# One step for a head pair's sums over values, and one pool of four PSUM banks for experts and values

## Chip, cores and metric

The kernel runs on one core of one Trainium2 chip. The metric is the device time of one execution in microseconds. Before the change three runs took 910.35, 912.54 and 912.85 us, a median of 912.54 us.

## What is computed

Eight batches of eight heads, 576 positions, head size 64. Causal attention with a decay that is summed from `f`; its rows go, 512 values per position (8 heads of 64), into a layer that takes the largest of three products and multiplies it by a fourth matrix. Cut to what matters:

```python
scores = q @ k.T / sqrt(64) + cum[i] - cum[j]        # cum = cumsum(log(clip(f)))
attn   = softmax over j <= i of scores               # 64 heads (8 batches x 8), 576 x 576
out    = attn @ v
x      = out laid out as 4608 tokens x 512
h      = max(x @ w1, x @ w2, x @ w3)                 # 512 -> 768
result = h @ w_out                                   # 768 -> 512
```

## The kernel before

**A plan writes the order.** Nothing is run as it is written. Every piece of work is handed to `Plan.add` (line 68) as a step: an engine, a cost in nanoseconds, a function that issues its instructions, the keys it reads and writes, and a priority. `Plan.emit` (line 87) then plays the steps through a model of the five engines: each engine takes, of the steps whose inputs are ready, the one with the lowest rank (priority less a small weight for the work that hangs on it). The order in which steps begin in that model is the order in which their instructions are issued. On the chip the engines run these queues in order, and semaphores on the data hold them. Steps of TensorE may carry two marks: `short` (a score pass whose last block is so narrow that the weight load behind it is not covered by it) and `light` (a step whose weights are 64 columns wide). After a `short` step the model looks for a `light` one (lines 117 to 128).

**Scores.** `scores` (line 646) handles a head in two units: unit 2 is the first 256 queries, unit 1 the other 320 (`UNITS`, line 610). In each, keys are on the partitions and queries on the columns, in blocks of up to 128 keys. A pass A (TensorE, line 675) fills the unit's PSUM banks, VectorE and GpSimd find a maximum (lines 730 to 748), a pass B (line 675 again) subtracts it, ScalarE takes exponentials (line 763) into a buffer of probabilities. Batch 0 (n below 8) has a form of its own that the change leaves as it is. Heads 8 to 15 have two such buffers for each unit, later heads three (`probs`, line 641).

**Values.** From head 8 on, two heads make a pair. `values` calls `values_pair` (line 820) once for unit 1 and once for unit 2, 28 pairs and so 56 steps. A step multiplies the probabilities of both heads by their values: the two heads fill the upper and the lower 64 partitions of one PSUM bank, `t` (`TPS`, line 373), with weights 64 columns wide, so that the two heads' matmuls run side by side (line 831). Unit 1 takes 20 matmuls, unit 2 takes 8. ScalarE copies the bank to `u` (line 858), and the other unit waits for that copy, since there is one bank. For heads 8 to 15 the row sums are taken in the same bank by a further step of 32-column matmuls (line 850) and copied by line 856; for later heads GpSimd sums them (line 787). `finish_pair` (line 942) divides: small DMAs through `sc` and `rdram` spread the reciprocal of the sums over a tile `r`, and VectorE multiplies `u` by it (line 961). When a batch is done `split_x` (line 963) writes its four `u` tiles as a high part (ScalarE, line 966) and a low part (VectorE, line 968).

**Experts.** `moe` runs batch b's layer while batch b+1's attention runs. `gemm1` (line 980) makes a group of 12 matmuls of 256 or 320 columns (line 992) for each of the three matrices; ScalarE copies the first (line 999), VectorE takes the maximum with the other two (line 1001), then the result is split (lines 1004, 1006). `gemm2_part` (line 1015) makes a group of 18 matmuls (line 1021), which ScalarE copies to `o` (line 1028). A group takes the next of three banks `mp0` to `mp2` in turn:

```python
def next_mp():                       # line 975
    i = mcount[0] % NM               # NM = 3
    mcount[0] += 1
    return MPS[i], f"mp{i}"
```

All transfers go through SyncE's queue, in the order of the plan.

Of the kernel before, what the change touches and what calls it, by code (L numbers as in the profile page):

```python
# [47 lines left out]

class Plan:
# [15 lines left out]
    def __init__(self):  # L65
        self.steps, self.wrote, self.read, self.parts = [], {}, {}, {}

    def add(self, eng, cost, fn, r=(), w=(), prio=0.0, xfer=0.0, rows=128, short=0.0, light=False):
# [16 lines left out]
        self.steps.append((eng, cost, fn, deps, prio, xfer, rows, short, light))  # L85

    def emit(self):
# [22 lines left out]
        clock = GatedClock()  # L110
        while done < n:
            best = None
            for e in free:
                t = free[e] if live[e] else (max(free[e], wait[e][0][0]) if wait[e] else None)
                if t is not None and (best is None or t < best[0]):
                    best = (t, e)
# [5 lines left out]
            here = live[e][0]  # L122
            if e == "PE" and (short or self.steps[here[1]][8]):


                x = min((x for x in live[e] if (self.steps[x[1]][8] if short else not self.steps[x[1]][8])), default=here)
                if x[0] < here[0] + (self.LIKE if short else self.HOLD):
                    here = x
# [9 lines left out]
            begin[i] = t  # L138
            cost = (self.steps[i][1] - saved) * self.ROOM[e][0] + self.ROOM[e][1]
# [5 lines left out]
            if self.steps[i][5]:  # L145
                moved = max(moved, end + 650) + self.steps[i][5]
                end = moved + self.LATE
                lanes.append(end + 650)
            for u in users[i]:
# [31 lines left out]
def kernel(  # L181
# [15 lines left out]
    nc = tc.nc  # L197
# [148 lines left out]
    def ZR():  # L346
        return lazy("rx", [P, 384], F32)
# [442 lines left out]
    def values(n, unit, prio):  # L790
# [26 lines left out]
        if j:  # L817
            values_pair(n, unit, prio)

    def values_pair(n, unit, prio):  # L820

        pi, d, t, kt = n // 2, UNITS[unit], TPS, "t0"
        u = pi % NU
        q0, nq, cols = d["q0"], d["nq"], d["cols"]
        vn, kv = VN[vbuf(pi)], f"vn{vbuf(pi)}"
        prs = [probs(n - 1, unit), probs(n, unit)]
# [8 lines left out]
        wide = n < WIDE  # L835
        add("PE", sum(4.04 * x[2] / 2.4 for x in cols) + 250, go, [k for _, k in prs] + [kv], [kt], prio, light=True)
        if wide:

            half, z0 = nq // 2, nq
            runs = [[(max(qa, half * a), min(qa + w, half * a + half), col - qa) for c, qa, w, col in cols] for a in range(2)]  # L840
            runs = [[x for x in xs if x[0] < x[1]] for xs in runs]

            def total():
                for x in range(max(map(len, runs))):
                    for j in range(2):
                        for a in range(2):
                            if x < len(runs[a]):
                                qa, qe, col = runs[a][x]
                                r = 64 * j + 32 * a
                                nc.tensor.matmul(  # L850
                                    t[r:r + 32, z0 + qa - half * a:z0 + qe - half * a], ZR()[:, 288:320],
                                    prs[j][0]()[:, col + qa:col + qe], start=False, stop=True, skip_group_check=True)

            add("PE", max(sum(4.04 * (x[1] - x[0]) / 2.4 for x in xs) for xs in runs) + 100, total,
                [k for _, k in prs] + ["ones", kt], [kt], prio)
            add("ACT", act_cost(half), lambda: nc.scalar.activation(
                ZR()[:, 128 * (2 - unit):128 * (2 - unit) + half], t[:, z0:z0 + half], AF.Copy), [kt], [f"zr{unit}"], prio)
        add("ACT", act_cost(nq), lambda: nc.scalar.activation(
            U(u)[:, q0:q0 + nq], t[:, 0:nq], AF.Copy), [kt], [f"u{u}/{unit}"], prio)
# [114 lines left out]

    def next_mp():
        i = mcount[0] % NM
        mcount[0] += 1
        return MPS[i], f"mp{i}"

    def gemm1(b, c0, cn, fb, parts, prio):  # L980
# [4 lines left out]
        for i in range(3):  # L985
            mp, km = next_mp()
            m = mp[:, 0:cn]
            for kt in range(KT):
                def go(kt=kt, i=i, m=m):
                    hh, ll = (xa(kt), xb(kt)) if early else (xh(kt)[:, c0:c0 + cn], xl(kt)[:, c0:c0 + cn])  # L990
                    for x, (w, xx) in enumerate(((0, hh), (0, ll), (1, hh))):
                        nc.tensor.matmul(  # L992
                            m, unit_w(i, fb)[:, w, kt, :], xx,
# [3 lines left out]
                    ([f"xa{kt}", f"xb{kt}"] if early else [f"xh{kt}", f"xl{kt}"]) + key_w(i, fb) + ([km] if kt else []), [km], prio)  # L997
            if i == 0:
                add("ACT", act_cost(cn), lambda m=m: nc.scalar.activation(t, m, AF.Copy), [km], [kt_], prio)  # L999
# [15 lines left out]
    def gemm2_part(hh, hl, kh, kl, col, row, c0, cn, prio):  # L1015
        mp, km = next_mp()
        cs, ds = slice(col, col + P), slice(c0, c0 + cn)
        for fb in range(FT):
            def go(fb=fb):
                for x, (l, r) in enumerate(((hh(), 0), (hh(), 1), (hl(), 0))):  # L1020
                    nc.tensor.matmul(  # L1021
                        mp[:, 0:cn], l[:, fb, cs], unit_o(fb)[:, r, ds],
# [3 lines left out]
                [kh + str(fb), kl + str(fb)] + key_o(fb) + ([km] if fb else []), [km], prio)  # L1026
        ko = "o" if cn == DM else f"o/{c0}"
        add("ACT", act_cost(cn), lambda: nc.scalar.activation(result()[:, ds], mp[:, 0:cn], AF.Copy), [km], [ko], prio)
# [29 lines left out]

    LEAD, MLAG, WP, WR = 2.1, -0.1, 0.7, 0.65
# [49 lines left out]
    lag = 0  # L1109
    moe(0, lambda x: H + lag + H * x)  # L1110
# [13 lines left out]
    for n in range(H, BH):  # L1124
# [10 lines left out]
        for unit in order:  # L1135
            values(n, unit, p + VO)
# [39 lines left out]
```

## Time and profile before

| | |
|---|---|
| runs | 910.35, 912.54, 912.85 us; median 912.54 us |
| profiled execution | span 909.0 us from its first to its last instruction, the one time of its own that the profile gives; the three runs stand 1.3 to 3.8 us above that span, the median 3.5 us |
| TensorE | busy 892.6 us, 98% of the span |
| VectorE, GpSimd, ScalarE | 69%, 48% and 42% |
| TensorE clock | mean of the granted clock 0.998 |

The span is what the trace can explain, and the rest lies around it. A busy TensorE is not one that works at its best: matmuls overlap, and a gap of some tens of nanoseconds between the starts of two of them is not shown as idle. So the start times of single matmuls are read beside the busy share. The first 120 us are mostly batch 0's attention and the preparation of weights, the last 80 us are the last batch's experts alone.

### The profile page before, as it was taken

To read this page: it belongs to the slowest core of one execution; us is meant where nothing else is said; L and a number is where in the kernel's file an instruction comes from. 1 tells how busy PE (TensorE), PEld (TensorE's weight loads), DVE (VectorE), ACT (ScalarE), POOL (GpSimd) and SP (SyncE) were. 2 spreads that over 40 slices of the span, in tenths; PEclk is the share of its full clock that TensorE was granted. 3 is DMA by queue.
4 is the path that set the end of the run, shared out by engine and by line. 5 is a ranking of instruction groups with operands and counts; after the bars stand their busy time and mean duration, and the time that the engine had idled before them with its cause. 6 is when DMAs were issued, how large, how long until landed. Compare 5 with 4: busy or idle time off the path is not lost.

```text
span 909.0 us, 18296 instructions
## 1 busy us (share of the span) xinstructions
PE 892.6 (98%) x6646; PEld 806.0 (89%) x6646; DVE 625.6 (69%) x1386; ACT 385.9 (42%) x882; POOL 432.1 (48%) x380
## 2 busy tenths in 40 slices
PE   8889999998999999999999999999999999999998
PEld 6789988887989998988989898998989898998998
DVE  6999564666859786786948877796957778672211
ACT  6896443443334443344434443444434443442111
POOL 4655134225465655646454755556456465650000
PEclk9999999999999999999999999999999999999999
DMA  7991255455454455446435544545444564401000
GB/s 202 364 259 43 70 158 139 123 133 150 94 131 132 124 131 140 134 92 172 101 101 139 137 140 109 156 94 139 123 112 131 117 156 113 109 14 37 1 35 24
DMA packets 93371, 110.99 MB, mean 122 GB/s; under 512 B 52461, under 2 KB 56301, under 8 KB 93282
## 3 DMA queue, kind: packets, MB, share of 16 engines
q1 hardware_dynamic: 93282, 109.83, 45.8%
q8 instruction: 53, 0.87, 0.4%
q14 instruction: 36, 0.29, 0.1%
HBM read 50.22 MB, written 9.87 MB: 66 GB/s over the span
## 4 chain that ended last, share of the span: by engine, by line
PE 88%; DVE 3%; ACT 2%; DMA 1%; issue 1%; POOL 1%; SPq 0%; DVEq 0%; ACTq 0%
PE mp L992 48%; PE mp L1021 16%; PE s L675 12%; PE t L831 9%; PE t L800 1%; PE t L850 1%; DVE hl L564 1%; POOL gm L745 1%; DMA vn<-in_v_dram 1%; DVE va_s L779 0%; DMA r_r<-rdram 0%; ACT w L501 0%; DVE mx L735 0%; DVE hdl_r L1006 0%; DVE tm L1001 0%
## 5 line engine op out<-in xcount | busy, mean ns | idle before, releaser
L992 PE MATMUL mp<-xh_r,w_r 128*128 128x320 f32 (+1 forms) x2160 | 463.9, 299 | 4.2 <-ACT xh_r L966 2.7
L992 PEld LDWEIGHTS mp<-xh_r,w_r 128*128 128x128 f32 x2160 | 356.6, 189 | 14.1 <-issue 5.6
L992 PE MATMUL mp<-xl_r,w_r 128*128 128x320 f32 (+1 forms) x1080 | 320.1, 296 | 0.4 <-DVE xl_r L968 0.4
L787 POOL PARTITION_ALL_REDUCE z<-va_s x96 | 194.8, 2029 | 161.9 <-DVE va_s L779 59.7
L745 POOL PARTITION_ALL_REDUCE gm<-mx x131 | 161.1, 1232 | 207.6 <-DVE mx L732 77.2
L992 PEld LDWEIGHTS mp<-xl_r,w_r 128*128 128x128 f32 x1080 | 203.6, 189 | 1.1 <-DVE xl_r L968 0.6
L1001 DVE TENSOR_TENSOR tm<-mp,tm 128x256 f32<-128x256 f32 (+1 forms) x192 | 86.4, 450 | 82.7 <-PE mp L992 76.8
L675 PEld LDWEIGHTS s<-qs_r,ks_r 128*128 128x128 f32 (+1 forms) x784 | 117.3, 182 | 19.5 <-issue 13.8
L675 PE MATMUL s<-qs_r,ks_r 128*128 128x320 f32 (+4 forms) x784 | 133.6, 286 | 0.3 <-POOL qs_r L748 0.3
L1021 PE MATMUL mp<-w_r,hmh_r 128*128 128x512 f32 (+1 forms) x396 | 122.8, 392 | 0.0
L735 DVE TENSOR_TENSOR mx<-mx,s 128x320 f32<-128x320 f32 (+3 forms) x248 | 92.2, 372 | 21.4 <-PE s L675 7.3
L1004 ACT ACTIVATE hmh_r<-tm 128x256 fp32r<-128x256 f32 x96 | 39.9, 415 | 105.3 <-DVE tm L1001 104.8
L1021 PEld LDWEIGHTS mp<-w_r,hmh_r 128*128 128x128 f32 x396 | 70.2, 188 | 13.4 <-issue 1.6
L1021 PE MATMUL mp<-w_r,hml_r 128*128 128x512 f32 (+1 forms) x198 | 76.8, 388 | 0.0
L564 DVE STREAM_TRANSPOSE hl<-hl 128x576 f32<-128x576 f32 x56 | 68.3, 1240 | 10.5 <-DMA hl<-in_k_dram 8.5
L999 ACT ACTIVATE tm<-mp 128x256 f32<-128x256 f32 (+1 forms) x96 | 39.6, 412 | 75.8 <-PE mp L992 71.3
L763 ACT ACTIVATE pf<-s 128x512 f32<-128x512 f32 (+4 forms) x107 | 49.1, 505 | 31.9 <-PE s L675 26.3
L1006 DVE TENSOR_TENSOR hml_r<-tm,hmh_r 128x256 fp32r<-128x256 f32 x96 | 49.2, 513 | 17.0 <-ACT hmh_r L1004 16.3
L704 DVE TENSOR_TENSOR s<-s,mask 128x256 f32<-128x256 f32 x96 | 41.0, 427 | 27.1 <-PE s L675 26.9
L748 POOL CAST qs_r<-gm 1x256 fp32r<-1x256 f32 (+1 forms) x112 | 55.5, 497 | 7.1
L763 ACT ACTIVATE ph_f<-s 128x384 f32<-128x384 f32 x80 | 36.1, 504 | 41.8 <-PE s L675 41.8
L742 ACT ACTIVATE mx<-s 128x320 f32<-128x320 f32 (+1 forms) x64 | 26.7, 416 | 60.5 <-DVE s L709 46.0
(213 smaller groups left out, 1224.6 us busy)
## 6 DMA issues: line engine op xcount, KB each, us to landing
qs_r<-hl SPq DMA_DIRECT2D x168, 144.0 KB
ks_r<-hl SPq DMA_DIRECT2D x168, 144.0 KB
w<-in_moe_w_dram SPq DMA_DIRECT2D x9, 1024.0 KB
out_dram<-o_r SPq DMA_DIRECT2D x35, 256.0 KB
hl<-in_q_dram SPq DMA_DIRECT2D x14, 576.0 KB
hl<-in_k_dram SPq DMA_DIRECT2D x14, 576.0 KB
r_r<-rdram SPq DMA_DIRECT2D x56, 144.0 KB
vn<-in_v_dram SPq DMA_DIRECT2D x30, 128.0 KB
```

The lines of the kernel that those rows point to most:

```text
L564: add("DVE", 1085, lambda e=e, tt=tt, xs=xs: nc.vector.transpose(tt[:, e], xs[:, e]), [key + "0"], [key + "1"], prio)
L675: nc.tensor.matmul(bank[bk][0:l.shape[-1], col:col + w], l, rhs(qa, w), start=start and bk not in begun, stop=stop, skip_group_check=True)
L735: nc.vector.tensor_tensor(mt[:, a:a + w], mt[:, a:a + w], bank[bk][:, col:col + w], op=ALU.max)
L745: add("POOL", 450 + 2.6 * nq, lambda: nc.gpsimd.partition_all_reduce(gm, mt, P, bass.bass_isa.ReduceOp.max), [km, km + "a"], [kg], prio - CB)
L748: add("POOL", 130 + 0.9 * nq, lambda: nc.gpsimd.tensor_copy(QS(s)[96:97, 1, q0:q0 + nq], gm[96:97, :]), [kg], [kx], prio - CB)
L763: add("ACT", act_cost(w), lambda bk=bk, w=w, col=col: nc.scalar.activation(px()[:, col:col + w], bank[bk][:, 0:w], AF.Exp, scale=sc), [kb[ ...
L787: add("POOL", 520 + 5.1 * nq, lambda: nc.gpsimd.partition_all_reduce(Z[:, q0:q0 + nq], blocks_sum()[:, q0:q0 + nq], P, bass.bass_isa.Reduc ...
L831: nc.tensor.matmul(t[D * j:D * j + D, qa:qa + w], vn[:, j, c, 0:D], prs[j][0]()[:, col:col + w], start=x == 0, stop=True, skip_group_check ...
L992: nc.tensor.matmul(m, unit_w(i, fb)[:, w, kt, :], xx, start=kt == 0 and x == 0, stop=kt == KT - 1 and x == 2,)
L1001: add("DVE", dve_cost(cn), lambda m=m: nc.vector.tensor_tensor(t, m, t, op=ALU.max), [km, kt_], [kt_], prio)
L1006: add("DVE", dve_cost(w), lambda hh=hh, hl=hl, a=a, d=d, w=w: nc.vector.tensor_tensor(hl()[:, fb, d:d + w], t[:, a:a + w], hh()[:, fb, d:d ...
L1021: nc.tensor.matmul(mp[:, 0:cn], l[:, fb, cs], unit_o(fb)[:, r, ds], start=fb == 0 and x == 0, stop=fb == FT - 1 and x == 2,)
```

## The change

A pair's two units become one step. It takes two banks, issues unit 2's 8 matmuls and then unit 1's 20, and the copies (and, for heads 8 to 15, the row sums) follow. The four banks `mp0`, `mp1`, `mp2` and `t` become one pool once batch 0's attention is through with them (`Plan.lend`). A step names the banks that it takes (`take`) and those that it gives back (`drop`): an expert group takes one at its first matmuls, a pair takes two at once, and the step that copies a bank out gives it back. Which bank it is, is settled when the model begins the step: the one that has been open longest. A TensorE step that finds too few open banks is passed over. Three smaller edits go with it: the copies of expert groups get a priority that is lower by 2 (`EV`), which puts them ahead on ScalarE and VectorE; groups begin in the order in which they are written (the key `turn`); and in the plan a `gemm1` group begins when all four parts of its input are split, not the first alone. The number of matmuls, copies and transfers stays.

```diff
+    def lend(self, key):
+        self.owed.append(set(self.read.get(key, ())) | ({self.wrote[key]} if key in self.wrote else set()))
...
+        def fits(i, t):
+            return not self.steps[i][9] or sum(x <= t for x in open_at) >= len(self.steps[i][9])
...
+            able = [x for x in live[e] if fits(x[1], t)]
+            if not able:
+                free[e] = t
+                continue
+            here = min(able)
             if e == "PE" and (short or self.steps[here[1]][8]):
...
             begin[i] = t
+            for slot in self.steps[i][9]:
+                slot.bank = min((x, bank) for bank, x in enumerate(open_at))[1]
+                open_at[slot.bank] = never
...
+            back = end + self.LAG[e][0] + self.MORE[0] if e in ("ACT", "DVE") else end
...
+            for slot in self.steps[i][10]:
+                open_at[slot.bank] = back
...
-    def values_pair(n, unit, prio):
-        pi, d, t, kt = n // 2, UNITS[unit], TPS, "t0"
+    def values_pair(n, prio):
+        pi = n // 2
...
+        slots = {1: Slot(), 2: Slot()}
+        kt = {x: f"av{pi}/{x}" for x in slots}
+        prs = {x: [probs(m, x) for m in (n - 1, n)] for x in slots}
         def go():
-            for x, (c, qa, w, col) in enumerate(cols):
-                for j in range(2):
-                    nc.tensor.matmul(
-                        t[D * j:D * j + D, qa:qa + w], vn[:, j, c, 0:D], prs[j][0]()[:, col:col + w],
-                        start=x == 0, stop=True, skip_group_check=True)
+            for x in (2, 1):
+                t = BANKS[slots[x].bank]
+                for y, (c, qa, w, col) in enumerate(UNITS[x]["cols"]):
+                    for j in range(2):
+                        nc.tensor.matmul(
+                            t[D * j:D * j + D, qa:qa + w], vn[:, j, c, 0:D], prs[x][j][0]()[:, col:col + w],
+                            start=y == 0, stop=True, skip_group_check=True)
-        add("PE", sum(4.04 * x[2] / 2.4 for x in cols) + 250, go, [k for _, k in prs] + [kv], [kt], prio, light=True)
+        add("PE", 4.04 * 1600 / 2.4 + 250, go, [k for x in prs for _, k in prs[x]] + [kv], list(kt.values()), prio, light=True,
+            take=tuple(slots.values()))
+        for unit in (2, 1):
...
+            add("ACT", act_cost(nq), lambda t=t, nq=nq, unit=unit: nc.scalar.activation(
+                U(u)[:, Q0[unit]:Q0[unit] + nq], t()[:, 0:nq], AF.Copy), [kt[unit]], [f"u{u}/{unit}"], prio, drop=(slots[unit],))
...
-    def next_mp():
-        i = mcount[0] % NM
-        mcount[0] += 1
-        return MPS[i], f"mp{i}"
+    BANKS = MPS + [TPS]
...
+                add("PE", 3 * mm_cost(cn, P), go,
+                    [c + str(x) for x in (range(kt, kt + 1) if kt else range(KT)) for c in (("xa", "xb") if early else ("xh", "xl"))]
+                    + key_w(i, fb) + ([km] if kt else []), [km] if kt else [km, "turn"], prio,
+                    take=() if kt else (slot,))
...
-                add("DVE", dve_cost(cn), lambda m=m: nc.vector.tensor_tensor(t, m, t, op=ALU.max),
-                    [km, kt_], [kt_], prio)
+                add("DVE", dve_cost(cn), lambda m=m: nc.vector.tensor_tensor(t, m(), t, op=ALU.max),
+                    [km, kt_], [kt_], prio + EV, drop=(slot,))
...
+    EV = -2.0
...
+    for key in ("mp0", "mp1", "mp2", "t0"):
+        plan.lend(key)
...
-        for unit in order:
-            values(n, unit, p + VO)
+        if n % 2:
+            values_pair(n, p + VO)
```

## Rows read from the trace of the kernel before

**Rows 1.** The page: its first line, busy time by engine (us, share of the span, instructions), and the chain of work that ended last, by engine and by line.

```profile
span 909.0 us, 18296 instructions
...
PE 892.6 (98%) x6646; PEld 806.0 (89%) x6646; DVE 625.6 (69%) x1386; ACT 385.9 (42%) x882; POOL 432.1 (48%) x380
...
PE 88%; DVE 3%; ACT 2%; DMA 1%; issue 1%; POOL 1%; SPq 0%; DVEq 0%; ACTq 0%
PE mp L992 48%; PE mp L1021 16%; PE s L675 12%; PE t L831 9%; PE t L800 1%; PE t L850 1%; DVE hl L564 1%; POOL gm L745 1%; DMA vn<-in_v_dram 1%; DVE va_s L779 0%; DMA r_r<-rdram 0%; ACT w L501 0%; DVE mx L735 0%; DVE hdl_r L1006 0%; DVE tm L1001 0%
```

**Rows 2.** Busy time in four stretches. Columns: the stretch and its length in us, busy us of PE, PEld, DVE, ACT and POOL (with instructions), the mean granted clock, DMA share, GB/s.

```profile
207.00:215.00 8.00, 4.90 (x23) 4.52 (x22) 3.62 (x8) 2.48 (x6) 4.32 (x4) 0.79 0.33 93
216.00:396.00 180.00, 180.00 (x1306) 162.98 (x1305) 140.00 (x317) 72.84 (x170) 100.25 (x82) 1.00 0.51 131
396.00:398.50 2.50, 1.16 (x8) 0.89 (x7) 2.40 (x5) 0.44 (x1) 2.18 (x1) 1.00 0.97 211
398.50:820.00 421.50, 421.36 (x2999) 379.36 (x3001) 315.16 (x726) 173.84 (x407) 239.53 (x193) 1.00 0.46 118
```

**Rows 3.** TensorE and ScalarE in order of time: start, length (us), line, operation, count, and in brackets the idle time before it with its releaser.

```profile
209.99 0.42 PE L992 MATMUL mp<-xh_r,w_r 128*128 128x320 f32 x1 [2.73 <-ACT xh_r L966]
210.78 0.52 PE L992 MATMUL mp<-xl_r,w_r 128*128 128x320 f32 x1 [0.38 <-DVE xl_r L968]
...
397.98 0.44 ACT L999 ACTIVATE tm<-mp 128x320 f32<-128x320 f32 x1 [3.85 <-DVE hdl_r L1006]
```

**Rows 4.** TensorE in order of time around a step of unit 1, with experts' matmuls of 256 columns on both sides; start, length (us). Of a pair of heads the one that starts first is shown.

```profile
343.60 0.28 PE L992 MATMUL mp<-xl_r,w_r 128*128 128x256 f32 x1
343.72 0.28 PE L992 MATMUL mp<-xh_r,w_r 128*128 128x256 f32 x1
343.93 0.27 PE L831 MATMUL t<-pl_f,vl 128*64 128x64 f32 x1
...
344.04 0.22 PE L831 MATMUL t<-pl_f,vl 128*64 128x64 f32 x1
...
344.09 0.33 PE L831 MATMUL t<-pl_f,vl 128*64 128x192 f32 x1
...
345.50 0.43 PE L831 MATMUL t<-pl_f,vl 128*64 128x320 f32 x1
...
345.77 0.43 PE L831 MATMUL t<-pl_f,vl 128*64 128x320 f32 x1
...
346.14 0.39 PE L992 MATMUL mp<-xh_r,w_r 128*128 128x256 f32 x1
346.36 0.28 PE L992 MATMUL mp<-xl_r,w_r 128*128 128x256 f32 x1
```

**Rows 5.** ScalarE's copies of the values' bank: duration in ns (least, median, most), first and last start, shapes.

```profile
L858 ACT ACTIVATE u<-t x44: 365/419/440, 146.6 to 823.8; 128x320 f32<-128x320 f32 x22, 128x256 f32<-128x256 f32 x22
L858 ACT ACTIVATE u_r<-t x12: 379/400/439, 124.0 to 770.3; 128x320 f32<-128x320 f32 x6, 128x256 f32<-128x256 f32 x6
```

**Rows 6.** TensorE in order of time where a score pass of unit 2 (blocks of 256 and 128 columns) and one of unit 1 (320, 320, 192, 64 and 320 columns) stand between expert groups of 320 columns. Blocks of a pass are shown as one row, with the first one's shape.

```profile
378.17 0.34 PE L675 MATMUL s<-qs_r,ks_r 128*128 128x256 f32 x2
378.35 0.36 PE L992 MATMUL mp<-xh_r,w_r 128*128 128x320 f32 x1
378.55 0.31 PE L992 MATMUL mp<-xl_r,w_r 128*128 128x320 f32 x1
...
379.28 0.81 PE L675 MATMUL s<-qs_r,ks_r 128*128 128x320 f32 x5
379.93 0.31 PE L992 MATMUL mp<-xh_r,w_r 128*128 128x320 f32 x1
```

**Rows 7.** TensorE in order of time: the first and the last of the 34 steps of values whose start follows a score pass's 64- or 128-column block directly (12 follow one of 64, 22 one of 128).

```profile
216.25 0.57 PE L675 MATMUL s<-qs_r,ks_r 128*128 128x320 f32 x4
216.75 0.27 PE L831 MATMUL t<-ph_f,vn 128*64 128x64 f32 x1
...
790.43 0.58 PE L675 MATMUL s<-qs_r,ks_r 128*128 128x320 f32 x4
790.93 0.27 PE L831 MATMUL t<-pf,vn 128*64 128x64 f32 x1
```

**Rows 8.** The chain of waits in order of time, from the last pair of batch 1 to the first expert matmuls of that batch: start, length (us), what.

```profile
185.00 0.27 PE t L831 x2
185.26 1.33 PE t L850 x32
186.60 3.72 PE mp L992 x24
190.32 0.80 PE t L831 x8
...
192.18 0.57 PE t L850 x12
...
205.08 3.23 DMA r_r<-rdram
...
210.78 0.79 PE mp L992 x2
```

**Rows 9.** ScalarE in order of time around the two copies of another pair.

```profile
373.31 0.44 ACT L858 ACTIVATE u_r<-t 128x320 f32<-128x320 f32 x1 [0.92 <-PE t L831]
...
376.65 0.38 ACT L858 ACTIVATE u_r<-t 128x256 f32<-128x256 f32 x1 [1.72 <-PE t L831]
```

More of the change, by code (lines that the diff above doesn't have):

```diff
@@ L46, in run @@
             self.turn()
+class Slot:
+    bank = None
 class Plan:
@@ L66, in __init__, with add @@
         self.steps, self.wrote, self.read, self.parts = [], {}, {}, {}
-    def add(self, eng, cost, fn, r=(), w=(), prio=0.0, xfer=0.0, rows=128, short=0.0, light=False):
+        self.owed = []
+    def lend(self, key):
+        self.owed.append(set(self.read.get(key, ())) | ({self.wrote[key]} if key in self.wrote else set()))
+    def add(self, eng, cost, fn, r=(), w=(), prio=0.0, xfer=0.0, rows=128, short=0.0, light=False, take=(), drop=()):
         i = len(self.steps)
@@ L84, in add @@
         deps.discard(i)
-        self.steps.append((eng, cost, fn, deps, prio, xfer, rows, short, light))
+        self.steps.append((eng, cost, fn, deps, prio, xfer, rows, short, light, take, drop))
     def emit(self):
@@ L110, in emit, with moment @@
         clock = GatedClock()
+        never = float("inf")
+        open_at = [never if x else 0.0 for x in self.owed]
+        owed = {}
+        for bank, x in enumerate(self.owed):
+            for i in x:
+                owed.setdefault(i, []).append(bank)
+        owe, last = [len(x) for x in self.owed], [0.0] * len(self.owed)
+        def fits(i, t):
+            return not self.steps[i][9] or sum(x <= t for x in open_at) >= len(self.steps[i][9])
+        def moment(e):
+            if not live[e]:
+                return max(free[e], wait[e][0][0]) if wait[e] else None
+            if e != "PE" or any(fits(i, free[e]) for _, i in live[e]):
+                return free[e]
+            later = [x for x in open_at if free[e] < x < never] + [max(free[e], x) for x, _ in wait[e][:1]]
+            return min(later, default=None)
         while done < n:
@@ L120, in emit @@
                 heapq.heappush(live[e], (rank[i], i))
[L122 removed]
+            able = [x for x in live[e] if fits(x[1], t)]
[3 more added lines that the diff above has]
+            here = min(able)
             if e == "PE" and (short or self.steps[here[1]][8]):
[L126 removed]
+                x = min((x for x in able if (self.steps[x[1]][8] if short else not self.steps[x[1]][8])), default=here)
                 if x[0] < here[0] + (self.LIKE if short else self.HOLD):
@@ L148, in emit @@
                 lanes.append(end + 650)
+            back = end + self.LAG[e][0] + self.MORE[0] if e in ("ACT", "DVE") else end
+            for bank in owed.get(i, ()):
+                owe[bank] -= 1
+                last[bank] = max(last[bank], back)
+                if not owe[bank]:
+                    open_at[bank] = last[bank]
+            for slot in self.steps[i][10]:
+                open_at[slot.bank] = back
             for u in users[i]:
@@ new lines, in values_pair, with total @@
+        add("PE", 4.04 * 1600 / 2.4 + 250, go, [k for x in prs for _, k in prs[x]] + [kv], list(kt.values()), prio, light=True,
+            take=tuple(slots.values()))
+        for unit in (2, 1):
+            nq, cols = NQ[unit], UNITS[unit]["cols"]
+            t = lambda unit=unit: BANKS[slots[unit].bank]
+            if wide:
+                half, z0 = nq // 2, nq
+                runs = [[(max(qa, half * a), min(qa + w, half * a + half), col - qa) for c, qa, w, col in cols] for a in range(2)]
+                runs = [[x for x in xs if x[0] < x[1]] for xs in runs]
+                def total(runs=runs, t=t, half=half, z0=z0, unit=unit):
+                    for x in range(max(map(len, runs))):
+                        for j in range(2):
+                            for a in range(2):
+                                if x < len(runs[a]):
+                                    qa, qe, col = runs[a][x]
+                                    r = 64 * j + 32 * a
+                                    nc.tensor.matmul(
+                                        t()[r:r + 32, z0 + qa - half * a:z0 + qe - half * a], ZR()[:, 288:320],
+                                        prs[unit][j][0]()[:, col + qa:col + qe], start=False, stop=True, skip_group_check=True)
+                add("PE", max(sum(4.04 * (x[1] - x[0]) / 2.4 for x in xs) for xs in runs) + 100, total,
+                    [k for _, k in prs[unit]] + ["ones", kt[unit]], [kt[unit]], prio)
+                add("ACT", act_cost(half), lambda t=t, half=half, z0=z0, unit=unit: nc.scalar.activation(
+                    ZR()[:, 128 * (2 - unit):128 * (2 - unit) + half], t()[:, z0:z0 + half], AF.Copy), [kt[unit]], [f"zr{unit}"], prio)
+            add("ACT", act_cost(nq), lambda t=t, nq=nq, unit=unit: nc.scalar.activation(
+                U(u)[:, Q0[unit]:Q0[unit] + nq], t()[:, 0:nq], AF.Copy), [kt[unit]], [f"u{u}/{unit}"], prio, drop=(slots[unit],))
```

45 lines of the change are left out of this document (11 added, 34 removed).

## The prediction

> **What bounds the kernel now.** I read the page first: TensorE is busy 98% of the span of 909.0 us, and 88% of the chain that ended last lies on it, expert matmuls (lines 992 and 1021) before score passes (675) and values (831, 9%) [rows 1]. The next engine, VectorE, stands at 69%. Then the stretches: from 216 to 396 us and from 398.5 to 820 us TensorE has no idle time but 0.14 us, so in the middle of the kernel nothing but less TensorE time can make it shorter [rows 2]. Third, the few real stalls. At 207 us, where batch 1's experts should begin, TensorE waits 2.73 and 0.38 us for the split of the input [rows 3]; the mean granted clock of 207 to 215 us is 0.79, so TensorE was for a time at 1.2 GHz instead of 2.4 [rows 2]. At 396 us it is idle for 1.34 us [rows 2], while ScalarE's copy of an expert bank waits for VectorE's line 1006 [rows 3]. Last, single matmuls in order of time, because a busy share of 98% doesn't tell what TensorE loses between matmuls of different kinds, and that is where this change acts.
>
> **The switch to values and back.** Around a step of unit 1 [rows 4] expert matmuls of 256 columns start 0.12 us apart. The first matmul of values starts 0.21 us after the last of them: 0.09 lost. The first pair of matmuls takes 0.11 us, the second, of the same shape, 0.05: 0.06 lost. The last pair takes 0.37 us, the one before it, of the same shape, 0.27: 0.10 lost. The first expert matmul after it takes 0.22 us instead of 0.12: 0.10 lost. One visit costs 0.35 us beside its own work, all of it on the engine that sets the end. I use 0.34, the mean that the unrounded starts of steps of both units give. There are 56 copies of values, 44 and 12 [rows 5], so 56 visits; after the change 28. The step issues all 28 matmuls from one function, so no plan can part them, and that the change doesn't do this is no case. 28 x 0.34 = **9.5 us** saved.
>
> From the rule "TensorEngine Tiling (Array Packing)" of the Trainium skill, section Key Properties, a change of tiling mode drains TensorE, and "TensorE: Matmul & The Clock Gate", section Step-by-step, puts a drain at about 128 cycles. By these pages one drain each way is an estimated 2 x 53 ns, the saving 28 times that, 3.0 us, and the time about 907. The trace agrees that a change of mode costs, but at three times this size.
>
> **What the join costs inside.** No row shows unit 2's last matmul (256 columns) followed by unit 1's first (64 columns). Within a step a change of width from 64 to 192 columns shows no gap (344.04 to 344.09 us is the pace of 64 columns) [rows 4]; the worst is the 0.06 of a first pair. I take 0, the nearest row, and keep 28 x 0.06 = 1.7 us as an end.
>
> **The cover that is lost.** After a score pass of unit 2 the next expert matmul takes 0.20 us instead of 0.15, 0.05 lost; after one of unit 1 the pass of 1,216 columns takes 0.65 us, against 1,216 / 320 x 0.147 = 0.56: 0.09 lost [rows 6]. A step of values behind such a block pays its own entry but not this. 34 of the 56 steps stand so, 22 at 0.05 and 12 at 0.09 [rows 7]: 2.2 us are covered now. With 28 steps at most 28 x 0.065 = 1.8 us are, and with the share of now, 61%, 1.1. Loss 0.4 to 1.1, I take **0.8 us**.
>
> **Batch 1's boundary.** The stall at 207 us ends a chain that begins with values [rows 8]: unit 1 of the batch's last pair and its row sums end at 186.6 us, then come 24 expert matmuls (3.72 us), and only at 190.3 us unit 2, whose row sums end at 192.75; behind them the DMAs of the division (the last one lands at 208.3), the multiplication, the split. Unit 2 needed the bank that unit 1 held, then lost its turn. As one step with two banks, unit 2's 0.64 us of matmuls come ahead of unit 1's, and both row sums can be done at about 187.8 us, 5 us earlier. TensorE arrives 4 pairs x 0.34 = 1.4 us earlier at the boundary, so the chain gains 3.6 us on it, more than the 3.1 us of waiting. The transfers keep their order on SyncE's queue only as far as the plan keeps it: an earlier `sc` transfer moves ahead of loads of `qs` and `ks` and of output stores, which belong to later heads. The ends are 0 (the chain is held by another queue) and 3.1 plus the clock's share, 8 x 0.21 = 1.7 us, together 4.8. I take **3.1 us**: the wait closes, but what is left of it may still be enough to lower the clock.
>
> **The pool.** Experts have four banks where they had three, save while a pair holds two. A pair holds them for its matmuls, some 2.7 us in which no expert group starts, and then until ScalarE has copied both, 0.44 and 0.38 us one after the other [rows 5, 9], about 1 us more with the hand-over. In that time the group in hand goes on in the third bank (12 matmuls at 0.12 to 0.15 are 1.4 to 1.8 us) and a fourth is there. I cost it at nothing; the cover is gone where VectorE is late with that fourth bank by a microsecond, and then TensorE waits. The other side is the stall at 396 us, where a fourth bank and copies of higher rank would have helped: 0 to 1.3 us gained, I take 0 and keep it for the range.
>
> **The small edits** cost nothing that runs: `turn` and the wait for all four parts exist in the plan alone, and the chip waits as before for data and banks. `EV` puts expert copies ahead of VectorE's maxima of scores: a few copies of the order of 0.4 us (ScalarE's of the same width take that [rows 5]) ahead of a head's chain, with a head every 12.5 us (28 pairs from 124 to 824 us [rows 5]); expert matmuls hide it as long as these last. What would be late next is a pair's division at the end of a batch. Copies, transfers and GpSimd's work keep their numbers; no transfer is added on any queue.
>
> **Sum.** 9.5 - 0.8 + 3.1 = 11.8 us off the profiled span of 909.0: 897.2. The median of the runs stands 3.5 us above that span; 912.5 - 11.8 = **900.7 us**.
>
> **Rivals.** *Only the visits go* (about 904): the boundary at 207 us keeps its wait, since SyncE's queue and not the values sets when the division runs, and the sum is 9.5 - 0.8 = 8.7 us. For it: in the chain the DMA part from 192.8 to 208.3 us is longer than the part on TensorE [rows 8]. Against it: its first link is the second visit.
>
> *Gain given back* (about 911, within 0.3%, or 2.7 us, which is about what a measurement of this kernel can tell from no change): a new order of the whole plan brings a wait like that of 396 us, 1.3 us, at five of the six later boundaries or a second one like 207 us with its clock, 4.8 us: 8.7 less 6 to 8. Against it: the long stretches without idle time show that there is other work nearly always [rows 2].
>
> *Slower through starved banks* (about 922): after each pair experts run on two banks until ScalarE has copied, and every group there waits for a VectorE or ScalarE copy that stands behind a longer operation. In its own words the Trainium skill's page "TensorEngine Tiling (Array Packing)", section PSUM Bottleneck, warns of this: tiles speed up TensorE and not the copying out of PSUM, which may become the bottleneck. The row at 396 us shows the price of one such wait, 1.3 us [rows 2, 3]; at one for half of the pairs it is 14 x 1.3 = 18 us, against 8.7 saved, so 9 to 10 slower. It decides from 8.7 / 28 = 0.31 us of waiting per pair, and shows as slower from 0.41. Against it: VectorE has 31% to spare, and with one bank for values and three for experts only one such wait shows in 600 us.
>
> **How the numbers follow.** My forecast, the visits and most of the boundary, gets 0.55; only the visits 0.30; gain given back 0.07; slower 0.08. The range takes in the bounds: at best 9.5 - 0.4 + 4.8 + 1.3 = 15.2 us, 897.3; with a microsecond more if the row sums of batch 1, now parted from their pair by other work in some places [rows 8], follow it directly, 896. At worst within the first two cases 9.5 - 1.7 - 1.1 = 6.7, 905.8; with a new stall like that at 396 us or two, 908.5. Faster by over 0.3% 0.85, within 0.3% 0.07, slower 0.08.
>
> **What would show it.** In the changed profile every step of values should be one run of 28 matmuls, 28 in all, entered and left with the same four losses; TensorE's busy time should fall by about 9 us with the same 6,646 matmuls; the stretch around 205 us should lose its idle time and its lowered clock; between boundaries TensorE should still not idle. I am wrong if TensorE's idle time grows by more than 9 us, with ScalarE or VectorE copies (lines 858, 999, 1001) as what it waits for, or if the entry into unit 1 costs as much inside the joined step as before.

## The result: 0.5% slower, and where the forecast gain went

Five runs after the change took 914.84 to 917.57 us, median 917.31; five of the kernel before 910.21 to 912.85, median 912.23. The ratio is **1.0053 [1.0035, 1.0070]**: slower by 0.35 to 0.70%, where 1.3% faster was forecast. The profiled execution of after is the lowest of its five, 914.84 us with a span of 912.7, so the two traces differ by 3.7 us of the 5.1 us between the medians.

The page of after, its parts 1 and 4 (busy us, share of the span, instructions; the chain by engine):

```profile
span 912.7 us, 18383 instructions
...
PE 886.5 (97%) x6646; PEld 807.3 (88%) x6646; DVE 623.9 (68%) x1386; ACT 382.8 (42%) x882; POOL 432.6 (47%) x380
...
PE 82%; DVE 8%; ACT 3%; DMA 2%; issue 2%; SPq 1%; POOL 1%; DVEq 0%; ACTq 0%; POOLq 0%
```

Against [rows 1] TensorE is busy 6.1 us less for the same 6,646 matmuls, as it should be, and yet the span is longer: its idle time grew from 16.4 to 26.2 us, by 9.8 us. VectorE's share of the chain rose from 3 to 8%. Stretches of after, beside [rows 2] (first column the stretch, then its length and busy us of PE, PEld, DVE, ACT, POOL, then the granted clock):

```profile
207.10:217.30 10.20, 4.94 (x26) 4.44 (x28) 6.87 (x15) 2.07 (x5) 7.14 (x5) 0.51 0.56 147
216.00:396.00 180.00, 177.44 (x1289) 161.61 (x1288) 134.15 (x308) 70.83 (x166) 101.29 (x83) 1.00 0.50 127
398.50:820.00 421.50, 419.62 (x3016) 382.13 (x3015) 316.94 (x729) 172.15 (x409) 238.36 (x194) 1.00 0.47 120
```

The first stretch ran at 0.51 of the clock, that is nearly all of it at 1.2 GHz, with TensorE idle for half of it. The two long stretches, which had 0 and 0.14 us of idle time, now have 2.56 and 1.88. What TensorE waits for (us in total, times, longest; the waits that are new or longer):

```profile
PE s L721 <- POOL qs_r L794: 7.4, 3, 6.2
PE s L721 <- ACT pf L809: 2.9, 4, 1.6
PE mp L1039 <- ACT tm L1048: 2.5, 3, 1.1
...
PE mp L1039 <- DVE tm L1050: 0.7, 1, 0.7
```

**The long wait**, TensorE of after in order of time (start, length, line, shape, idle time and releaser in brackets), to be read beside [rows 3]:

```profile
204.58 1.08 PE L721 MATMUL s<-qs_r,ks_r 128*128 128x320 f32 x7 [0.81 <-ACT ph_f L809]
205.50 0.36 PE L1039 MATMUL mp<-xh_r,w_r 128*128 128x320 f32 x1
205.70 0.31 PE L1039 MATMUL mp<-xl_r,w_r 128*128 128x320 f32 x1
205.84 0.31 PE L1039 MATMUL mp<-xh_r,w_r 128*128 128x320 f32 x1
212.36 1.86 PE L721 MATMUL s<-qs_r,ks_r 128*128 128x320 f32 x7 [6.21 <-POOL qs_r L794]
```

and the chain that releases it (start, length, what):

```profile
204.05 0.82 ACT ph_f L809 x2
...
204.89 0.50 DVE va_s L822
...
206.72 2.15 POOL z L833
...
209.91 1.69 POOL gm L791
...
211.65 0.66 POOL qs_r L794
...
212.36 1.76 PE s L721 x6
```

The wait of 2.73 us on the split of the input is now one of 6.21 us on the next head's maximum. Exponentials, sums and maxima come too late: attention of batch 1 has fallen behind, and behind only three expert matmuls the queue holds a score pass. Before, 27 expert matmuls ran from 202.91 us on, up to a score pass just ahead of the wait. What holds attention up shows some 30 us earlier, on ScalarE, at the exponentials of head 14 (after, then before):

```profile
174.10 1.80 ACT L809 ACTIVATE pf<-s 128x512 f32<-128x512 f32 x4 [3.31 <-PE mp L901]
...
170.87 1.69 ACT L763 ACTIVATE pf<-s 128x512 f32<-128x512 f32 x4 [2.33 <-PE s L675]
```

Before, they wait for their scores. In after they wait for the row sums (line 901) of the late pair of heads 12 and 13, which still reads the buffer that head 14 needs.

**A short wait**, VectorE and ScalarE of after before TensorE's wait at 243.8 us:

```profile
241.03 1.92 DVE L825 TENSOR_TENSOR va_s<-va_s,ph_f 128x320 f32<-128x320 f32 x3
242.87 0.42 DVE L1055 TENSOR_TENSOR hml_r<-tm,hmh_r 128x256 fp32r<-128x256 f32 x1
243.20 1.41 DVE L1055 TENSOR_TENSOR hdl_r<-tm,hdh_r 128x64 fp32r<-128x64 f32 x1
...
244.72 0.44 ACT L1048 ACTIVATE tm<-mp 128x320 f32<-128x320 f32 x1 [3.73 <-DVE hdl_r L1055]
...
245.21 0.41 PE L1039 MATMUL mp<-xh_r,w_r 128*128 128x320 f32 x1 [1.08 <-ACT tm L1048]
```

ScalarE stands idle for 3.73 us at a copy that `EV` has put ahead, and waits for the tile `tm`: the subtraction that frees the tile (line 1055, no `EV`) waits its turn on VectorE behind a head's sums (825). The bank stays full, and TensorE idles.

**The joined step** does what it says. One of after, beside [rows 4] (TensorE in order of time, of the two heads the one that starts first):

```profile
246.31 0.69 PE L721 MATMUL s<-qs_r,ks_r 128*128 128x128 f32 x5
246.93 0.32 PE L879 MATMUL t<-pf,vl 128*64 128x128 f32 x1
...
247.41 0.38 PE L879 MATMUL t<-pf,vl 128*64 128x256 f32 x1
...
247.63 0.22 PE L879 MATMUL mp<-pf,vl 128*64 128x64 f32 x1
...
249.42 0.43 PE L879 MATMUL mp<-pf,vl 128*64 128x320 f32 x1
...
249.79 0.42 PE L721 MATMUL s<-qs_r,ks_r 128*128 128x320 f32 x1
```

Unit 2's last matmul and unit 1's first (247.41 to 247.63 us) stand 0.22 us apart, the pace of 256 columns: the join costs nothing inside. There are 28 such runs of 28 matmuls.

**A ledger.** Each matmul is given the usual distance to the next start for its shape; what lies over it is lost. Against before, in us:

| term | forecast | after | e7 (below) |
|---|---|---|---|
| visits to values (95.2 us with their own work) | -9.5 | -8.4 | -9.8 |
| score passes, lost cover | +0.8 | +2.1 | +1.0 |
| waits over 0.4 us, from 120 us on | -3.1 | +7.8 | -0.4 |
| everything before 120 us | 0 | +2.9 | +0.7 |
| not placed | 0 | -0.7 | -0.3 |
| span | -11.8 | +3.7 | -8.8 |

The visits came nearly as forecast. The waits rose from 5.5 us (four) to 13.3 us (nine; 6.4 of it the long one). **The pairs are late**: from a pair's last exponential to its first matmul pass 5.08 us in the mean and 13.4 at most; before, unit 1 began after 2.07.

### The profile page after: what moved, and what is told of

The parts are those of the page before. It is cut to its first block, busy times and chain, and to the rows that moved or that the text cites. A ratio compares the mean times of both kernels' runs of the same rounds, so it can differ in the third digit from the quotient of the medians.

```text
span 912.7 us, 18383 instructions
## 1 busy us (share of the span) xinstructions
PE 886.5 (97%) x6646; PEld 807.3 (88%) x6646; DVE 623.9 (68%) x1386; ACT 382.8 (42%) x882; POOL 432.6 (47%) x380
## 4 chain that ended last, share of the span: by engine, by line
PE 82%; DVE 8%; ACT 3%; DMA 2%; issue 2%; SPq 1%; POOL 1%; DVEq 0%; ACTq 0%; POOLq 0%
PE mp L1039 34%; PE t L1039 11%; PE mp L1070 11%; PE s L721 11%; PE mp L879 7%; PE t L1070 5%; PE t L879 2%; DMA w<-in_moe_w_dram 1%; PE t L846 1%; DVE va_s L825 1%; POOL gm L791 1%; SPq L426 1%; DVE mx L781 1%; DVE hl L610 1%; DVE mx L778 1%
## 5 line engine op out<-in xcount | busy, mean ns | idle before, releaser
L1039 PE MATMUL mp<-xh_r,w_r 128*128 128x320 f32 (+1 forms) x1616 | 384.1, 299 | 3.2 <-ACT tm L1048 2.5
L1039 PEld LDWEIGHTS mp<-xh_r,w_r 128*128 128x128 f32 x1616 | 279.1, 188 | 7.9 <-ACT tm L1048 3.2
L1039 PE MATMUL mp<-xl_r,w_r 128*128 128x320 f32 (+1 forms) x808 | 239.3, 296 | 0.0
L1039 PEld LDWEIGHTS mp<-xl_r,w_r 128*128 128x128 f32 x808 | 152.3, 188 | 0.5
L1039 PE MATMUL t<-xh_r,w_r 128*128 128x320 f32 (+1 forms) x544 | 150.7, 297 | 0.0
L1050 DVE TENSOR_TENSOR tm<-mp,tm 128x256 f32<-128x256 f32 (+1 forms) x147 | 66.5, 453 | 59.0 <-PE mp L1039 42.2
L1039 PEld LDWEIGHTS t<-xh_r,w_r 128*128 128x128 f32 x544 | 101.4, 188 | 0.9 <-DVE hml_r L1055 0.5
L1070 PE MATMUL mp<-w_r,hmh_r 128*128 128x512 f32 (+1 forms) x276 | 84.4, 388 | 0.0
L1039 PE MATMUL t<-xl_r,w_r 128*128 128x320 f32 (+1 forms) x272 | 80.3, 295 | 0.0
L1053 ACT ACTIVATE hmh_r<-tm 128x256 fp32r<-128x256 f32 x96 | 40.0, 416 | 95.2 <-DVE tm L1050 94.9
L1070 PEld LDWEIGHTS mp<-w_r,hmh_r 128*128 128x128 f32 x276 | 48.6, 188 | 8.1 <-issue 0.2
```

The costliest lines, as they stand in the source:

```text
L1039: nc.tensor.matmul(m(), unit_w(i, fb)[:, w, kt, :], xx, start=kt == 0 and x == 0, stop=kt == KT - 1 and x == 2,)
L1070: nc.tensor.matmul(BANKS[slot.bank][:, 0:cn], l[:, fb, cs], unit_o(fb)[:, r, ds], start=fb == 0 and x == 0, stop=fb == FT - 1 and x == 2,)
```

## Experiments

Three causes were in question (the expectations name them in words or by these letters). **C**: a pair needs two open banks at one moment, expert groups take each bank as it opens, so the pair is passed over again and again, probabilities keep their buffers, attention falls behind. **E**: expert copies are ahead, but what frees their tile `tm` is not. **A**: the rule that a `gemm1` group begins with four split parts keeps experts out of gaps. The rival is that the joined step itself costs something. Every ratio is against the kernel before, run on the same chip. Kernels with the edit of e2 have 8 lines more (1056 is 1048 of after, 1058 is 1050, 1063 is 1055), e4 has one; the third tile shows as `rx_t`.

**e1.** A `gemm1` group may begin with the part that its first matmuls read, as before.

```diff
...
-    [c + str(x) for x in (range(kt, kt + 1) if kt else range(KT)) for c in (...)]
+    ([f"xa{kt}", f"xb{kt}"] if early else [f"xh{kt}", f"xl{kt}"])
...
```

> The changed kernel, but an expert group's first matmuls read one part of the input again, as before the change, in place of all four (in the plan; the chip's waits are the same). Against a fixed amount of matmul work TensorE has lost 2.9 us more than before by 120 us, where batch 0's attention leaves gaps that experts fill. Theory A (the four-part rule holds these experts back): the 2.9 us come back, experts start to fill at 47 us again, and the time is about 914.4 us. Rival B (the pool of banks opens too late for them): no change before 120 us, 917.3 us. Both: the wait at 205 us stays.

915.59 us against 910.82, 1.0039 [1.0014, 1.0063]. The wait at 206 us was expected to stay; it is one of 0.85 and one of 2.5 us now, though pairs are as late as in after (4.94 us). New waits of 2.3 and 2.2 us on `tm` come at 238 and 291 us. Before 120 us the loss is 45.5 us instead of 46.5 (43.6 before), and the clock explains what is left: e1 has two stretches of 3.4 us at 1.2 GHz there, near 12 and 43 us, which before doesn't have, and e8 (below), with before's order of instructions and two such stretches, loses 45.5 as well. So the 2.9 us are back. In time e1 can't be told from after, whose interval overlaps: alone, A is a part and not the cause.

**e2.** While a pair doesn't find two banks, steps that take a bank and stand behind the pair in rank (a higher number) are held.

```diff
...
+        held = [x for x in live[e] if len(self.steps[x[1]][9]) == 2 and not fits(x[1], t)]
+        if held:
+            able = [x for x in able if not self.steps[x[1]][9] or x < min(held)]
...
```

> The changed kernel, but while a pair is ready and finds fewer than two open banks, no expert group of higher rank number may take one: the banks are kept for the pair. Theory C (pairs come late because they need two banks at once and experts take each bank as it opens; late pairs hold the probabilities of heads 8 to 15, so batch 1 ends late and TensorE waits 6.4 us at 206 us with its clock lowered): the pair of heads 12 and 13 starts within 2 us of its last exponential instead of 5.6, the wait at 206 us falls below 3 us, and the time falls by 4 to 7 us to 910 to 913. Rival D (the joined step is late because it needs both units' exponentials and stands as one block ahead of score passes): nothing changes, 916 to 919 us.

913.00 us against 910.82, 1.0023 [1.0004, 1.0042]. Pairs begin after 3.43 us instead of 5.08, and from 195 to 215 us TensorE loses 1.55 us instead of 9.84: without C the long wait is gone. The times alone would not show it, since the interval touches that of after. New waits take its place, and they are E. Waits of TensorE, then VectorE and ScalarE ahead of the first of them:

```profile
PE mp L887 <- DVE tm L1058: 4.1, 3, 2.8
PE t L887 <- ACT tm L1056: 2.7, 1, 2.7
```

```profile
235.17 1.15 DVE L833 TENSOR_TENSOR va_s<-va_s,ph_f 128x320 f32<-128x320 f32 x3
236.24 0.42 DVE L1063 TENSOR_TENSOR hml_r<-tm,hmh_r 128x256 fp32r<-128x256 f32 x1
...
236.57 1.40 DVE L1063 TENSOR_TENSOR hdl_r<-tm,hdh_r 128x64 fp32r<-128x64 f32 x1
...
238.09 0.44 ACT L1056 ACTIVATE tm<-t 128x320 f32<-128x320 f32 x1 [5.03 <-DVE hdl_r L1063]
...
238.58 0.32 PE L887 MATMUL t<-pf,vl 128*64 128x128 f32 x1 [2.66 <-ACT tm L1056]
```

A pair waits for a bank whose copy waits for the tile whose subtraction is late.

**e3.** The pool as in after, but a pair is two steps with one bank each (unit 1 first).

```diff
...
-        add("PE", 4.04 * 1600 / 2.4 + 250, go, ..., take=tuple(slots.values()))
+        for unit in (1, 2):
+            add("PE", sum(4.04 * x[2] / 2.4 for x in UNITS[unit]["cols"]) + 250, lambda unit=unit: go(unit), ..., take=(slots[unit],))
...
```

> The changed kernel with its pool, its four-part rule and its rank for copies, but the two units of a pair are two steps again, each with one bank: 56 visits to values instead of 28, which by the trace cost 8.4 us more. Theory C (needing two banks at once is what makes pairs late): the wait at 206 us shrinks by 4 to 7 us, and the time is 917.3 + 8.4 - 5.5, about 920. If the pool and the rank of copies by themselves lose the time: 917.3 + 8.4, about 926. If everything that was lost, save the 2.9 us before 120 us, hangs on the join: 912.2 + 2.9, about 915.

919.38 us against 910.82, 1.0088 [1.0062, 1.0114]. The long wait is gone (0.98 us lost from 195 to 215 us) and the visits are back. So the pool alone doesn't make that wait. The kernel is 0.9% slower than before all the same, with the 56 visits of before and pairs no later than there (1.70 us in the mean).

**e4.** Pairs own two banks, experts the other two.

```diff
-            return not self.steps[i][9] or sum(x <= t for x in open_at) >= len(self.steps[i][9])
+            own = open_at[2:] if len(self.steps[i][9]) == 2 else open_at[:2]
+            return not self.steps[i][9] or sum(x <= t for x in own) >= len(self.steps[i][9])
...
```

> The changed kernel with the pool cut in two: pairs have two banks of their own, experts the other two. Theory C: pairs start within 1 us of being ready and batch 1's boundary loses its long wait; but experts with two banks wait for their copies. From the one such wait of before, 1.3 us with three banks, I expect 0.2 to 0.5 us at a good part of some 380 groups and a time of 930 to 990 us: that would show what the forecast's rival of starved banks costs when it does happen. Rival: experts do well with two banks, then the time is 908 to 912 us.

946.29 us against 910.82, 1.0378 [1.0349, 1.0407]. The pairs are prompt (1.14 us), and experts on two banks pay for it:

```profile
PE mp L1040 <- DVE tm L1051: 9.0, 16, 1.4
PE mp L1040 <- ACT tm L1049: 8.0, 17, 3.1
```

These two lines are 17.0 us of waiting; in all TensorE idles 39.8 us instead of 16.4 before. That is the rival "slower through starved banks" in pure form, 35 us dear. In after, at 917, the pairs starved and not the experts.

**e5.** after, with a third tile `tm` from batch 1 on (in a buffer that is free by then).

```diff
-        ti = tmc[0] % 2
+        ti = tmc[0] % (3 if b else 2)
-        t, kt_ = TM[ti][:, 0:cn], f"tm{ti}"
+        t, kt_ = (TM[ti] if ti < 2 else lazy("rx", [P, S1], F32, "t"))[:, 0:cn], f"tm{ti}"
...
```

> The changed kernel with a third tile tm for the experts' maximum from batch 1 on (it lies where the row sums of heads 8 to 15 lay). Theory E: in the middle TensorE now waits for banks (3.2 us, at 244, 294, 299 and 608 us) because ScalarE's copy of an expert bank needs a tile tm that VectorE has not yet read out (its subtraction, line 1055, stands behind the sums of probabilities), while the copies themselves have a rank two heads better. With a third tile these waits go: about 3 us, 914 us, and the waits for line 1048 fall below 1 us. Rival F: the waits come from too few banks, not from the tiles: unchanged, 917 us. Both: the 6.4 us at 206 us stay.

919.09 us against 910.25, 1.0094 [1.0064, 1.0125]. The waits on ScalarE's `tm` are gone, the long wait is still there, and pairs begin even later (7.02 us):

```profile
PE s L721 <- POOL qs_r L794: 9.0, 4, 6.6
...
PE mp L1039 <- DVE tm L1050: 1.9, 3, 1.0
```

E alone is refuted as the cause. That a freer tile lets experts take banks still faster is a reading of the later pairs, and no run tests it.

**e6.** e2 and e5 together.

> Banks kept for a ready pair (as in the second run) and the third tile tm. In the second run the wait at 206 us went (1.6 us lost between 195 and 215 us instead of 9.8), but two pairs then waited 2.7 and 2.8 us for an expert bank whose copy was held. Theories C and E together: both kinds go, 913.0 less 5.5, about 907.5 us, below the kernel before (910.8). If a ready pair with reserved banks only moves the waiting elsewhere (rival): 911 to 914.

**903.23** us against 910.25, 0.9904 [0.9870, 0.9938]. From 120 us on two waits over 0.4 us are left, 0.74 us at 206 and 0.84 us at 516 us. With C and E mended together the sign turns.

**e7.** e6 and e1 together.

> As the run before it, and an expert group's first matmuls again read one part of the input (theory A: 1 to 3 us before 120 us). Theories A, C and E together leave the 28 visits saved (8.4 us) and at most 2 us of lost cover, and the boundary at 207 us without its 5 us: 902 to 906 us. If a new wait takes their place: 909 or more.

**902.21** us against 910.25, **0.9894 [0.9857, 0.9932]**, the best here. The one-part rule shows as no more than 1.0 us over e6, inside the intervals. Its page, and three stretches of it:

```profile
span 900.2 us, 18348 instructions
...
PE 884.2 (98%) x6646; PEld 805.3 (89%) x6646; DVE 625.7 (70%) x1386; ACT 384.2 (43%) x882; POOL 427.5 (47%) x380
```

```profile
208.00:218.00 10.00, 9.47 (x75) 8.04 (x74) 7.22 (x19) 4.41 (x13) 7.39 (x6) 1.00 0.74 213
216.00:396.00 180.00, 177.32 (x1293) 161.39 (x1291) 139.21 (x311) 71.74 (x168) 101.19 (x82) 1.00 0.50 127
398.50:820.00 421.50, 421.48 (x3013) 383.23 (x3013) 313.51 (x721) 172.93 (x408) 236.74 (x192) 1.00 0.46 119
```

The boundary at 208 us is nearly closed and keeps its clock, and the later stretch has 0.02 us of idle time. From 216 to 396 us 2.68 us are idle, most of it waits on `tm` at 238, 342 and 395 us, so E is not quite gone.

**e8.** The kernel before with the third tile.

> The kernel before with the third tile tm alone: the plan gives the same order on every engine, so only waits for tm can go. They cost 1.3 us at 396 us there. Theory E: 0.5 to 1.5 us faster than before, about 909.8 against 910.8; the gain of the two runs above does not come from the tile by itself. Rival: the tile is worth several us in the kernel before as well, 905 to 907.

911.23 us against 910.25, 0.9992 [0.9967, 1.0017]. The tile is worth nothing there (the wait at 396 us stayed), so the gain of e6 and e7 is not the tile's alone.

**e9.** e7's tile and one-part rule, the pool, but two steps per pair as in e3.

> Third tile tm, one-part rule and pool as in the run at 902 us, but a pair's units as two steps with one bank each (nothing then needs two banks at once, so nothing is kept). If the gain of that run is the 28 visits saved (8.4 us in the trace): about 910.5 us, with 56 visits and no long wait at 206 us. If it comes from the pool and the tile: 902 to 904.

922.44 us against 911.82, 1.0110 [1.0093, 1.0128]; 910.5 had been expected. Of the 21.4 us of span over e7, visits are 11.5 (96.9 against 85.4 us), some of it at the lowered clock, and waits of over 0.4 us are 6.4. Some 2 us lie before 120 us, where the clock is at 1.2 GHz for 6.8 us from 11.4 us on. Most of the waiting is one new wait at a later boundary:

```profile
PE mp L1039 <- ACT xh_r L1017: 4.7, 1, 4.7
```

Without the join this plan has no gain, so the gain of e7 needs it. But with A, C and E out of the way and 56 visits the kernel should have come out level with before, and it is 11.9 us over what was expected: the three causes are not all that the new plan costs, and no run shows what the rest is.

**e10.** e7 without the kept banks.

> The run at 902 us without keeping banks for a ready pair. Theory C: pairs are late again by some 5 to 7 us after their last exponential in the mean (3.1 with the banks kept), the probabilities of heads 8 to 15 are held, and the boundary near 206 us loses its wait back: 908 to 914 us. If keeping banks only mattered together with the four-part rule: 902 to 905.

908.07 us against 911.82, 0.9954 [0.9936, 0.9972]. The wait and the lateness (5.30 us, at most 15.6) return, and the loss from 195 to 215 us is 5.8 us:

```profile
213.55 0.90 PE L721 MATMUL s<-qs_r,ks_r 128*128 128x320 f32 x2 [2.41 <-POOL qs_r L794]
```

C again, from the other side: 0.6 points of ratio. But the kernel is still faster than before, with its pairs as late as in after. It differs from e5 by the one-part rule alone, and from 1.0094 to 0.9954 that is 1.4 points; the wait near 206 us is 2.4 us instead of 6.6, as it fell from 6.2 to 2.3 between after and e1. So A with E turns the sign as C with E does, and late pairs by themselves do not make the kernel slow.

**e11.** e7 with two tiles; the split steps that free them (lines 1053 and 1055) get `EV` as well.

```diff
...
-    ... AF.Copy), [kt_], [kh + str(fb)], prio)
+    ... AF.Copy), [kt_], [kh + str(fb)], prio + EV)
-    [kt_, kh + str(fb)], [kl + str(fb)], prio)
+    [kt_, kh + str(fb)], [kl + str(fb)], prio + EV)
...
```

> As the run at 902 us, but two tiles tm, and the split of the maximum (lines 1053 and 1055, which read a tile tm out) gets the same better rank as the copies. If the waits for banks in the middle come from the copies being ranked ahead of the work that frees their tile, they go here as they do with a third tile: 902 to 905 us. If the third tile itself is needed: waits on the lines of the copies of 3 us and more, 906 to 909.

**902.48** us against 911.82, 0.9902 [0.9883, 0.9921]: as good as the third tile, and pairs begin after 2.72 us. The waits on `tm` at 238 and 342 us are gone. So order serves here as well as a buffer. What e7 would be with two tiles and the old ranks was not run, so what either is worth beside the other two edits isn't shown.

**e12.** e7 with `EV = 0`.

> As the run at 902 us, but the copies of expert groups keep the rank of their group (EV 0). If the better rank is what keeps four shared banks moving: copies come late, TensorE waits on them, 907 us or more. If it is neutral: 901 to 904. If it holds back the scores' maxima, as the forecast weighed: faster, 899 to 901.

910.17 us against 911.82, 0.9982 [0.9969, 0.9996]: 0.9 points of ratio lost against e7. Pairs wait for copies again:

```profile
PE mp L887 <- DVE rx_t L1058: 3.6, 2, 2.6
PE mp L1047 <- ACT o_r L1086: 1.8, 2, 1.1
```

## Why the prediction was wrong

**The visits: right.** 8.4 us saved in after, with one pair inside the lowered clock (215.88 to 219.61 us, 3.7 us instead of 2.8), and 9.8 in e7, against 9.5. The Trainium skill's "TensorEngine Tiling (Array Packing)", section Key Properties, with the drain of its "TensorE: Matmul & The Clock Gate", section Step-by-step, had led to an estimate of 3.0; both runs decide against that size. The join inside costs nothing, as taken.

**The cover: too small**, 2.1 us for 0.8, and above its upper end of 1.1; e7 has 1.0. In after part of it falls in the stretch at 1.2 GHz.

**The step that failed first: "The pool ... I cost it at nothing."** I asked what experts do while a pair holds two banks, and not how the pair gets two at one moment. Before, the values' bank was theirs alone; in the pool each opened bank goes to a one-bank step that fits at once. The pair slipped from 2.07 to 5.08 us after its inputs. In batch 1, where a unit has only two buffers of probabilities, that holds up the exponentials (3.31 us at head 14): the first matmuls of heads 14 and 15 came at 190.7 us (183.0 before), and at 205.8 us TensorE had nothing ready. e2 and e10 show it by taking the cause away and by putting it back. Its price hangs on the small edits: in e10 pairs are as late, and the wait is 2.4 us.

**So "Batch 1's boundary" had the wrong sign.** I had the joined step come earlier and close the wait, 3.1 us; the stretch from 195 to 215 us loses 9.84 us instead of 5.65, 4.2 more. The pair's row sums end at 196.2 us, where 187.8 was forecast and before had 192.8, and the last part of the input is split at 211.2 and 212.0 us (high and low part; 209.9 and 210.7 before): the chain that the step was to shorten is late too. With kept banks the forecast is right in kind: e2 loses 1.55 there, 4.1 less than before.

**"The small edits cost nothing that runs" failed too.** `EV` moves the copies but not the subtraction that frees their tile: waits of 0.7 to 1.25 us from 243.8 us on. I had looked for what `EV` delays (a head's chain), not for what the copies themselves wait on. Yet `EV` is needed: e12 loses 8 us without it. The four-part rule has a price too. Before 120 us after loses 2.9 us more than before, both at 2.4 GHz there; e5 and e6, which have the rule, lose 2.8 us more than e1 and e8, which don't, all four with the same two stretches at 1.2 GHz. And it makes the long wait longer, 6.2 us instead of 2.3 (e1) and 6.6 instead of 2.4 (e5 beside e10).

**The rivals.** "Slower through starved banks" had the sign and the pool, but the wrong victim: experts were to starve, and the one long wait is a score pass. Of the prediction's own signs, TensorE's idle time did grow by more than 9 us, but copies are what it waits for in 3.4 us only (1.3 before). "Gain given back" had the mechanism of a new order with new waits, and 911. With A, C and E mended the kernel comes to 902.2 and 902.5, ratios of 0.989 and 0.990, beside the 900.7 forecast, 0.987: the number needed a plan that keeps banks for the pair, and this one doesn't.

**Open**: what e3 and e9 lose without a pair that needs two banks; why e9 waits 4.7 us before 636 us (VectorE's multiplication by `r`, line 1012, starts at 634.6 us behind a head's sums and maxima, and the split follows it; that it could have gone first isn't shown); how much of the scattered 1 to 2 us waits in each kernel is chance of its order; and why the four-part rule, worth 1.4 points between e5 and e10, shows no difference between e6 and e7, where banks are kept.

## What to carry to other kernels

Who needs two units of a shared pool at once needs a claim on them, or single requests take each as it opens: ask of a new allocation who is passed over, and who waits for that one. A step that is put ahead can stand idle while the step that frees its output tile keeps its place. Faults of one plan don't add up: mended alone, A, C and E move the ratio by -0.1, -0.3 and +0.4 points, none of them clear of the noise, but A with E by -1.0, C with E by -1.5. And a wait that a change should close has to be followed past the work that moves, to the buffers that it holds.

## What was not expected of the hardware

VectorE's subtraction of 128x64 takes 0.218 us at the median of 48 and 1.41 us at 243.20 us; others take 1.40 at 236.57 us of e2 and, ahead of the stall of [rows 3], at 396.48 us of before. All three overlap an all-reduce of GpSimd, whose row for the first is

```profile
243.04 2.26 POOL L833 PARTITION_ALL_REDUCE z<-va_s  x1 [0.40 <-DVE va_s L825]
```

That is 1.2 us on the path that frees `tm`, as long as TensorE's wait there. Overlap alone is not enough: the next subtraction of 128x64 in after, at 244.87 us, takes 0.211 us inside the same all-reduce, 1.8 us after its start, and the three long ones start within 0.2 us of theirs. No run took the all-reduce away, so this is a reading and no proof. And the clock: in before it stood at 1.2 GHz for 3.4 us from 210.9 us on, 0.9 us behind the wait of 2.73 us; in after for 10.2 us from 207.4 us on, 1.2 us into the wait of 6.21 us and until 5.3 us behind its end. It isn't the same in every execution: before and e8 run the same TensorE instructions up to 120 us, with waits of 1.58 and 1.67 us ahead of 10.3 us and of 1.48 and 1.47 us ahead of 42.3 and 42.9 us; before's clock stays at 2.4 GHz there, e8's falls to 1.2 GHz for 3.4 us from 12.0 and from 42.7 us on, and e8 is 2.0 us later from there.
